# Sketched attention and a tanh feed-forward block on one core: engine orders from a searched table, w_out in 2 KB rows, part of the sketch set-up after the key projection

## The chip, the cores and the metric

The kernel runs on one core of a Trainium2 chip. The metric is the device time of one execution in microseconds (us); less is better. The kernel before was timed three times: 115.40, 114.22 and 115.14 us, median 115.14 us.

## What is computed

For each of 4 batches and 4 heads, with 1088 positions of 32 numbers, polynomial-sketch attention; its result, 4352 tokens of 128 numbers, goes through a feed-forward block of width 2048.

```python
def phi(x):                                   # r = 8, so 64 features
    a = np.einsum('rd,bhsd->bhsr', S1, x)
    b = np.einsum('rd,bhsd->bhsr', S2, x)
    return np.einsum('bhsi,bhsj->bhsij', a, b).reshape(*x.shape[:-1], r * r)
kv = np.einsum('bhsf,bhsd->bhfd', phi(k), v)
z = np.sum(phi(k), axis=2)
x = (phi(q) @ kv) / (phi(q) @ z + 1e-6)       # per head; heads side by side: 4352 x 128
h = x @ w_in                                  # 128 -> 2048
out = (h - np.tanh(h)) @ w_out                # 2048 -> 128
```

## The kernel before

Every operation is first recorded by `P.op` with an engine, an estimated cost, the tiles that it reads and writes, and a priority. `schedule` then simulates the five engines (TensorE = "tensor" or PE, ScalarE = "scalar" or ACT, VectorE = "vector" or DVE, GpSimd = "gpsimd" or POOL, SyncE = "sync" or SP) and puts each engine's operations in an order: of what is ready, the one of lowest priority number. `sync` puts semaphore waits between them. On the chip each engine runs its own list in that order, so an operation that waits holds up all that stand behind it on its engine.

The work has three layers. **Opening (batch 0).** Keys and queries are loaded, turned by DVE transposes (kT L496, qT L665), projected on PE with the sketch matrix psk (L503 "kproj", L685 "qproj"), and turned back (kab L515, qab L691). The outer products wk of the keys are formed on DVE and POOL (L555); PE sums them with v (L568 for batch 0, L637 for others). The denominators go through a fold (gram L523, zm L529, and either u0 at L730 or ufold L532 and u L703) and a DVE chain uT, dm, den, rden, qa; the outer products qp of the queries follow (L587, L786). PE turns qp (L602) and forms the numerators ("num": L619 for batch 0, in the pieces tiles 0, 1, 2-3, 4-7, 8; L809 for others), and ACT or DVE casts them into xT (L625, L819), which holds the tokens in bf16. **Weights.** w_in and w_out are loaded in four pieces each (L411, L416), cast to bf16 (w_in by ACT and POOL at L832, w_out by POOL at L836); w_in is turned on PE (L846, copied out by ACT at L851), and PE multiplies it with w_out into a 128 x 128 matrix, kept as whi and wlo ("wfold", L858). So h @ w_out needs only x times whi and wlo ("lin", L886). **Layers.** Ten windows of tokens (256, 256, seven of 512, 256) run over 16 blocks of the width 2048: PE multiplies xT with a block of w_in ("L1", L901), ACT takes tanh of two or four blocks at once, 1024 columns (L905, into one of 20 slots of tt), PE adds w_out times that into one PSUM bank ("L2", L914). At the end of a window DVE turns the bank (osb L920) and four to eight DMAs write it out. The hidden product uses PSUM banks 0 to 3 in two pairs; banks 1 to 3 serve the opening too: num of tiles 2-3 of batch 0 lies in bank 3 until DVE casts it into xT (L625, 128x256), and the second half of the fourth group of L1 needs that bank. Batches 1 to 3 of the attention are woven between the windows.

`schedule` also puts filler matmuls on PE (on the zero tile wz, L427 and L428), where PE would idle, from when the memset of wz (L426) stands in DVE's list until the first numerators.

## Time and profile before

| | |
|---|---|
| runs, us | 115.40, 114.22, 115.14 (median 115.14) |
| profiled execution, us | 114.93 |
| its span, first to last instruction, us | 113.1 |
| PE busy | 100.4 us, 89% |
| ACT busy | 76.3 us, 67% |
| DVE busy | 60.7 us, 54% |
| POOL busy | 35.6 us, 32% |

Times in the rows are us from the start of the span unless marked ns. In a timeline row the first number is the start, the second the time to the end of the last instruction of the group, xN the number of instructions, and the bracket the idle time of that engine just before and what ended it. Ends of matmuls are modelled, and matmuls overlap: "busy" of PE is more than its streaming. PEclk is the granted clock of PE as a share of 2.4 GHz.

### The profile page before, as it was taken

The numbers are of one execution on the slowest core, as the hardware profiler recorded it, in microseconds if no ns is written. First come the engines' busy times: TensorE is split into PE (matmuls) and PEld (weight loads), VectorE is DVE, ScalarE is ACT, GpSimd is POOL, SyncE is SP. The second block draws the span as 40 slices with busy tenths as digits, with TensorE's granted clock in tenths as the row PEclk, the third lists the DMA queues.
The fourth block names the chain that finished last, engine by engine and source line by source line (L and its number), as shares of the span: only waits on it lengthen the run. The fifth ranks groups of instructions, "written<-read, shape, count | busy, mean of one in ns | idle before, by whom it ended". The sixth has DMA issues, their size and how long they took to land.

```text
span 113.1 us, 2876 instructions
## 1 busy us (share of the span) xinstructions
PE 100.4 (89%) x1204; PEld 53.1 (47%) x1215; DVE 60.7 (54%) x150; ACT 76.3 (67%) x98; POOL 35.6 (32%) x43
## 2 busy tenths in 40 slices
PE   4999893599998979999999999999999989989770
PEld 3847552496546624343643434364344434335450
DVE  1679951997497973948973395398503020020210
ACT  3006395565543863949799677959977999999900
POOL 5528362040085850087670008729100000000000
PEclk9999999859999999999999999999999999999999
DMA  2999999400199311894300230060014033014053
GB/s 80 291 236 372 307 316 202 130 7 0 26 306 254 64 22 25 267 248 123 61 0 0 45 54 0 0 97 1 0 23 70 6 47 48 0 26 67 0 90 50
DMA packets 25724, 11.19 MB, mean 99 GB/s; under 512 B 18928, under 2 KB 23408, under 8 KB 25712
## 3 DMA queue, kind: packets, MB, share of 16 engines
q1 hardware_dynamic: 25136, 10.95, 40.8%
q8 instruction: 9, 0.15, 0.6%
q10 hardware_dynamic: 576, 0.07, 0.4%
q14 instruction: 3, 0.02, 0.1%
HBM read 8.78 MB, written 2.23 MB: 97 GB/s over the span
## 4 chain that ended last, share of the span: by engine, by line
PE 58%; DMA 13%; ACT 12%; DVE 6%; SPq 3%; issue 2%; POOL 2%; DVEq 0%
PE ps L901 20%; PE ps L914 18%; ACT tt L905 12%; DMA kraw<-in_k_dram 8%; DMA w_in_f<-in_moe_w_in_dram 5%; PE ps L809 4%; PE ps L886 4%; POOL qp L786 2%; PE ps L637 2%; DVE osb L920 2%; PE ps L703 2%; PE ps L685 2%; PE ps L503 2%; SPq L404 2%; PE ps L858 2%
## 5 line engine op out<-in xcount | busy, mean ns | idle before, releaser
L905 ACT ACTIVATE tt<-ps 128x1024 bf16<-128x1024 f32 (+1 forms) x70 | 66.2, 1003 | 14.1 <-PE ps L901 13.6
L901 PE MATMUL ps<-xT,w_in 128*128 128x512 bf16 (+1 forms) x155 | 40.8, 351 | 5.1 <-DVE xT L625 2.5
L914 PE MATMUL ps<-tt,w_out 128*128 128x512 bf16 (+1 forms) x154 | 38.4, 346 | 0.1
L555 POOL TENSOR_TENSOR wk<-kab 128x768 f32<-128x768 f32 (+2 forms) x11 | 15.7, 1423 | 27.6 <-DVE kab L515 24.3
L901 PEld LDWEIGHTS ps<-xT,w_in 128*128 128x128 bf16 x160 | 13.6, 98 | 21.1 <-ACT tt L905 9.2
L914 PEld LDWEIGHTS ps<-tt,w_out 128*128 128x128 bf16 x160 | 15.6, 99 | 14.4 <-issue 1.7
L920 DVE STREAM_TRANSPOSE osb<-ps 128x512 f32<-128x512 f32 (+1 forms) x10 | 6.3, 630 | 26.2 <-PE ps L914 19.2
L786 POOL TENSOR_TENSOR qp<-qa,qab 128x768 f32<-128x768 f32 x6 | 11.4, 1901 | 6.5 <-DVE qa L778 6.3
L792 DVE STREAM_TRANSPOSE qpT<-qp 128x768 f32<-128x768 f32 x9 | 8.8, 977 | 1.9 <-POOL qp L786 1.8
L496 DVE STREAM_TRANSPOSE kT<-kraw 128x576 f32<-128x576 f32 (+3 forms) x9 | 5.7, 663 | 2.4 <-DMA kraw<-in_k_dram 2.4
L819 DVE CAST xT<-ps 128x256 bf16<-128x256 f32 x6 | 2.5, 420 | 7.5 <-PE ps L809 7.5
L665 DVE STREAM_TRANSPOSE qT<-qraw 128x512 f32<-128x512 f32 (+1 forms) x8 | 5.6, 723 | 0.1
L819 ACT CAST xT<-ps 128x256 bf16<-128x256 f32 x6 | 2.2, 381 | 4.3 <-PE ps L809 4.3
L886 PE MATMUL ps<-xT,whi 128*128 128x512 bf16 (+1 forms) x10 | 3.5, 351 | 1.7 <-DVE osb L920 1.7
L809 PE MATMUL ps<-qpT,kvw 32*32 32x288 f32 (+1 forms) x192 | 4.6, 399 | 0.0
L691 DVE STREAM_TRANSPOSE qab<-ps 128x512 f32<-128x512 f32 (+1 forms) x5 | 3.0, 601 | 2.3 <-PE ps L685 2.2
L428 PE MATMUL ps<-wz 128*128 128x128 bf16 x25 | 3.2, 311 | 1.1 <-DVE pmask L443 1.1
L637 PE MATMUL ps<-wk,vx 128*32 128x64 f32 x216 | 3.6, 220 | 0.3 <-POOL wk L555 0.3
L637 PEld LDWEIGHTS ps<-wk,vx 128*32 128x32 f32 x216 | 3.2, 110 | 1.4 <-issue 1.4
L545 ACT COPY ps<-kab 128x128 f32<-128x128 f32 x1 | 0.3, 271 | 5.2 <-DVE kab L515 5.2
L836 POOL CAST w_out<-w_out_f 128x512 bf16<-128x512 f32 x4 | 2.5, 616 | 3.7 <-DMA w_out_f<-in_moe_w_out_dram 3.7
L886 PE MATMUL ps<-xT,wlo 128*128 128x512 bf16 (+1 forms) x10 | 3.5, 347 | 0.0
(110 smaller groups left out, 101.2 us busy)
## 6 DMA issues: line engine op xcount, KB each, us to landing
vx<-in_v_dram SPq DMA_DIRECT2D x8, 144.0 KB, 3.9
qraw<-in_q_dram SPq DMA_DIRECT2D x4, 288.0 KB, 5.6
qraw<-in_q_dram SPq DMA_DIRECT2D x4, 256.0 KB, 4.8
vx<-in_v_dram SPq DMA_DIRECT2D x8, 128.0 KB, 4.7
w_in_f<-in_moe_w_in_dram SPq DMA_DIRECT2D x4, 256.0 KB, 5.3
w_out_f<-in_moe_w_out_dram SPq DMA_DIRECT2D x4, 256.0 KB, 7.5
out_dram<-osb SPq DMA_DIRECT2D x16, 64.0 KB, 2.0
kraw<-in_k_dram SPq DMA_DIRECT2D x3, 288.0 KB, 2.7
```

Source lines behind the costliest of these rows:

```text
L496: P.op("vector", dve(hi - lo), lambda e, lo=lo, hi=hi: e.transpose(out=kT[:, lo:hi], in_=kraw[i][:, lo:hi]), r=cells("kraw", i, lo, hi), w ...
L555: P.op(eng, dve(cols) if eng == "vector" else pool2(cols), lambda e, t0=t0, t1=t1, ap=ap, m=m, ka0=ka0: e.tensor_tensor(out=wk[:, t0:t1, : ...
L637: ins = e.matmul(ps[32 * h:32 * h + 32, vb, 0:64], vx[i][:, h, t, :], wk[:, t, h, :, :], start=(t == 0), stop=(t == NT - 1), tile_position ...
L665: P.op("vector", dve(hi - lo), lambda e: e.transpose(out=qT[i][:, lo:hi], in_=qraw[i][:, lo:hi]), r=cells("qraw", i, lo, hi), w=cells("qT" ...
L786: P.op(eng, dve(cols) if eng == "vector" else pool2(cols), lambda e, p0=p0, p1=p1, w=w: e.tensor_tensor(out=qp[:, p0:p1, :, :, :].rearrang ...
L792: P.op("vector", dve(cols), lambda e, p0=p0, p1=p1: e.transpose(out=qpT[:, p0:p1, :, :, :].rearrange("p t h y j -> p (t h y j)"), in_=qp[: ...
L809: ins = e.matmul(ps[32 * h:32 * h + 32, nb[g], 0:32 * n], kvw[i][32 * g:32 * g + 32, y, 32 * h:32 * h + 32], qpT[32 * g:32 * g + 32, t0:t0 ...
L886: P.op("tensor", pe(n), lambda e, x=x: e.matmul(acc[:, 0:n], x[:, :], xT[:, f0:f0 + n], start=f0 > 0 and x is whi, stop=not f0 and x is wl ...
L901: P.op("tensor", pe(n), lambda e, jb=jb + y, y=y, hb=hb: e.matmul(hb[:, n * y:n * y + n], w_in[:, 128 * jb:128 * jb + 128], xT[:, f0:f0 + ...
L905: P.op("scalar", act(q * n), lambda e, un=un, hb=hb, q=q: e.activation(out=tt[:, un, 0:q * n], in_=hb[:, 0:q * n], func=AF.Tanh, scale=-1. ...
L914: P.op("tensor", pe(n), lambda e, jb=jb, un=un, y=y: e.matmul(acc[:, 0:n], w_out[:, jb, :], tt[:, un, n * y:n * y + n], start=(not f0 and ...
L920: P.op("vector", dve(n), lambda e: e.transpose(out=osb[u][:, 0:n], in_=acc[:, 0:n]), r=[ka], w=[("osb", u)], prio=slot0, name=f"osb{w}")
```

## The change

A table ORDER gives for each engine the numbers of the recorded operations in the order in which they run; `schedule` follows it and no longer chooses. Priorities and costs, several of which are changed too, no longer set an order; costs still decide where fillers go. In the vector list, operation 0, the memset of wz, is among the last entries (batch 3's part), and a filler may only be placed once it is listed; PE's list has none left (29 before). w_out is read so that a partition takes four consecutive rows (2 KB) instead of four rows 128 apart (512 bytes each); so that the product stays the same, the casts of w_in read their columns with a step of four. The mask and the matrix s2blk ("sketch", L456, L470, L459, L481 before) are made after the key projection. The fold of batch 0 comes after the sums. Of the copies of qpB, that of tile 1 moves to ACT and that of tiles 2-3 to DVE. No other arithmetic changes.

```diff
+ORDER = {
+    "tensor": (
+        "55 62 63 64 72 82 70 84 90 91 108 92 93 94 110 96 122 116 118 124 126 120 136 128 169 170 141 144 130 172 173 138 132 "
...
+    "vector": (
...
+        "494 518 515 517 0 514 519 520 521 522 532 533 531 575 529 535 602 604 603 633 680 731 775 "
...
+        turn = {}
+        for e, text in (ORDER or {}).items():
+            for x, i in enumerate(text.split()):
+                turn[self.ops[int(i)]] = x
...
+                if turn:
+                    o = min(avail[e], key=turn.get)
+                    t = max(free[e], o.ready)
...
     def load_w_out(prio):
         for x in range(4):
...
                 out=w_out_f[:, 4 * x:4 * x + 4, :],
-                in_=moe_w_out[512 * x:512 * x + 512, :].rearrange("(jb ji) c -> ji jb c", jb=4)))
+                in_=moe_w_out[512 * x:512 * x + 512, :].rearrange("(ji jb) c -> ji jb c", jb=4)))
...
     def casts(engs, gate):
...
-                w_in[:, 512 * x:512 * x + 512], w_in_f[:, 512 * x:512 * x + 512]),
+                w_in[:, 512 * x:512 * x + 512].rearrange("p (jb ji) -> p jb ji", jb=4),
+                w_in_f[:, 512 * x:512 * x + 512].rearrange("p (ji jb) -> p jb ji", jb=4)),
...
+    def folding(gate):
+        P.op("tensor", 60, lambda e: e.matmul(
+            ps[:, 6, 0:32], e4[:, :, :, :].rearrange("p a b c -> p (a b c)"), e4[:, 0, :, :].rearrange("p b c -> p (b c)"),
+            start=True, stop=True), r=[("e4",)], w=[bank[6]], prio=-898, mode="s", name="mask", ni=4, after=gate)
...
-    gram = keys(0, opening, (0, 1), 4)
+    gram = keys(0, opening, (0, 1), 4, then=folding)
...
+    key_fold(0, opening, 4, [summed])
...
-    x0 = numerators_first(first, [(1, 2, 3, "vector")], 6, "scalar")
+    x0 = numerators_first(first, [(1, 2, 3, "scalar")], 6, "scalar")
...
-    numerators_first(then, [(2, 4, 1, "scalar")], 3, "vector")
+    numerators_first(then, [(2, 4, 1, "vector")], 3, "vector")
```

**DVE, end of the opening.** Before, the transposes kT of batch 1's keys stand ahead of the cast of tiles 2-3 into xT (128x256):

```order
L665 STREAM_TRANSPOSE qT<-qraw 128x576
L691 STREAM_TRANSPOSE qab<-ps 128x2x4x2x16
L696 STREAM_TRANSPOSE qab<-ps 64x2x2x16
L711 STREAM_TRANSPOSE uT<-ps 128x128
L715 STREAM_TRANSPOSE uT<-ps 64x32
L496 STREAM_TRANSPOSE kT<-kraw 128x576
L625 CAST xT<-ps 128x256
L770 TENSOR_TENSOR dm<-qab,uT 128x20x8
L496 STREAM_TRANSPOSE kT<-kraw 128x512
```

and with the change (L552 is kT, L689 the cast, L651 qp):

```order
L729 STREAM_TRANSPOSE qT<-qraw 128x576
L673 COPY qpB<-ps 128x512
L755 STREAM_TRANSPOSE qab<-ps 128x2x4x2x16
L775 STREAM_TRANSPOSE uT<-ps 128x128
L760 STREAM_TRANSPOSE qab<-ps 64x2x2x16
L779 STREAM_TRANSPOSE uT<-ps 64x32
L834 TENSOR_TENSOR dm<-qab,uT 128x20x8
L837 TENSOR_REDUCE den<-dm 128x20
L689 CAST xT<-ps 128x256
L840 RECIPROCAL rden<-den 128x20
L842 TENSOR_TENSOR qa<-qab,rden 128x160
L651 TENSOR_TENSOR qp<-qa,qab 128x256
```

Both kT now stand behind these rows, so the cast no longer has a load of batch 1 ahead of it.

**POOL, casts of the weights.** Before, the four pieces of w_out are cast in the order of their loads (d_wo0 to d_wo3 are the semaphores of the pieces):

```order
L832 CAST w_in<-w_in_f 128x512 [waits s_gpsimd,s_scalar,d_wi2]
L832 CAST w_in<-w_in_f 128x512 [waits s_gpsimd,d_wi3]
L836 CAST w_out<-w_out_f 128x512 [waits s_gpsimd,d_wo0]
L836 CAST w_out<-w_out_f 128x512 [waits s_gpsimd,d_wo1]
L836 CAST w_out<-w_out_f 128x512 [waits s_gpsimd,d_wo2]
L836 CAST w_out<-w_out_f 128x512 [waits s_gpsimd,d_wo3]
```

and with the change (L896 casts w_in, L901 casts w_out):

```order
L896 CAST w_in<-w_in_f 128x512 [waits s_gpsimd,d_wi2,s_scalar]
L896 CAST w_in<-w_in_f 128x512 [waits s_gpsimd,d_wi3]
L901 CAST w_out<-w_out_f 128x512 [waits s_gpsimd,d_wo3]
L901 CAST w_out<-w_out_f 128x512 [waits s_gpsimd,d_wo2]
L504 MEMSET vx 64x4x32 [waits s_gpsimd]
L901 CAST w_out<-w_out_f 128x512 [waits s_gpsimd,d_wo0]
L901 CAST w_out<-w_out_f 128x512 [waits s_gpsimd,d_wo1]
```

The first cast now waits for the piece that is loaded last, and the piece that L2 needs first (d_wo0) comes third.

**PE, end of the program.** Before (L901 is L1, L886 lin, L914 L2; 128x256 is the last window):

```order
L901 MATMUL ps<-xT,w_in 128x256 x4
L914 MATMUL ps<-tt,w_out 128x512 x3
L901 MATMUL ps<-xT,w_in 128x256 x2
L914 MATMUL ps<-tt,w_out 128x512 x2
L901 MATMUL ps<-xT,w_in 128x256 x2
L886 MATMUL ps<-xT,whi 128x256
L886 MATMUL ps<-xT,wlo 128x256
L914 MATMUL ps<-tt,w_out 128x256 x16
```

and with the change (L966 is L1, L951 lin, L979 L2):

```order
L966 MATMUL ps<-xT,w_in 128x256 x4
L979 MATMUL ps<-tt,w_out 128x512 x3
L966 MATMUL ps<-xT,w_in 128x256 x6
L951 MATMUL ps<-xT,whi 128x256
L951 MATMUL ps<-xT,wlo 128x256
L979 MATMUL ps<-tt,w_out 128x256 x6
L966 MATMUL ps<-xT,w_in 128x256 x2
L979 MATMUL ps<-tt,w_out 128x256 x10
```

Six of the last window's sixteen L2 now stand ahead of its last two L1, ten behind them.

## Rows read from the trace of the kernel before

**Rows 1.** The head of the page: span, and busy time by engine.

```profile
span 113.1 us, 2876 instructions
PE 100.4 (89%) x1204; PEld 53.1 (47%) x1215; DVE 60.7 (54%) x150; ACT 76.3 (67%) x98; POOL 35.6 (32%) x43
```

**Rows 2.** The timeline, 19 to 25 us.

```profile
19.44 0.78 DVE L496 STREAM_TRANSPOSE kT<-kraw 128x576 f32<-128x576 f32 x1 [2.35 <-DMA kraw<-in_k_dram]
20.14 0.38 DVE L625 CAST xT<-ps 128x256 bf16<-128x256 f32 x1
20.59 0.83 PE L901 MATMUL ps<-xT,w_in 128*128 128x256 bf16 x6 [2.54 <-DVE xT L625]
...
22.92 1.91 PE L858 MATMUL ps<-w_out,w_inT 128*128 128x128 bf16 x16
```

**Rows 3.** Busy time by engine in stretches, with granted clock and DMA.

```profile
core 0: us, PE busy (x) PEld busy (x) DVE busy (x) ACT busy (x) POOL busy (x), PEclk, DMA share, GB/s
...
8.00:12.00 4.00, 4.00 (x119) 2.82 (x118) 3.84 (x15) 2.51 (x7) 3.28 (x5) 1.00 1.04 353
...
21.72:25.13 3.41, 3.04 (x23) 2.79 (x24) 3.31 (x8) 2.64 (x4) 1.55 (x2) 0.50 0.03 12
```

**Rows 4.** The timeline, 4 to 15 us, and one row at 29.7 us.

```profile
4.78 1.25 PE L428 MATMUL ps<-wz 128*128 128x128 bf16 x10
...
5.66 0.28 DVE L481 TENSOR_TENSOR s2blk<-ps,mask 128x128 f32<-128x128 f32 x1
...
5.95 1.19 PE L503 MATMUL ps<-kT,psk 64*32 64x288 f32 x16
...
13.13 0.42 DVE L609 COPY qpB<-ps 128x256 f32<-128x256 f32 x1
...
14.41 0.59 ACT L851 COPY w_inT<-ps 128x512 bf16<-128x512 bf16 x1
14.41 0.39 PE L901 MATMUL ps<-xT,w_in 128*128 128x256 bf16 x2
...
29.74 0.69 PE L503 MATMUL ps<-kT,psk 64*32 64x288 f32 x16
```

**Rows 5.** The timeline of POOL, 9 to 20 us.

```profile
10.96 1.36 POOL L832 CAST w_in<-w_in_f 128x512 bf16<-128x512 f32 x2 [0.36 <-DMA w_in_f<-in_moe_w_in_dram]
...
17.82 0.62 POOL L836 CAST w_out<-w_out_f 128x512 bf16<-128x512 f32 x1 [0.89 <-DMA w_out_f<-in_moe_w_out_dram]
```

**Rows 6.** DMA packets in 8:11 (w_in's) and in 12:14 (w_out's).

```profile
DMA packets 598, 1.08 MB, mean 358 GB/s; under 512 B 67, under 2 KB 91, under 8 KB 598
...
DMA packets 1185, 0.60 MB, mean 302 GB/s; under 512 B 36, under 2 KB 1184, under 8 KB 1184
```

**Rows 7.** The chain that ended last: start, us, what.

```profile
42.12 0.43 PE ps L914 x2
42.55 1.48 PE ps L809 x49
...
62.56 1.48 PE ps L809 x49
...
83.42 1.48 PE ps L809 x49
...
107.75 1.76 PE ps L914 x16
...
109.54 0.45 DVE osb L920
```

**Rows 8.** The timeline, 30 to 42 us.

```profile
30.74 0.67 DVE L515 STREAM_TRANSPOSE kab<-ps 128x512 f32<-128x512 f32 x1
...
40.87 0.39 PE L886 MATMUL ps<-xT,whi 128*128 128x512 bf16 x1 [0.75 <-DVE osb L920]
```

**Rows 9.** The timeline of ACT, 86 to 108 us.

```profile
86.33 14.14 ACT L905 ACTIVATE tt<-ps 128x1024 bf16<-128x1024 f32 x15 [0.61 <-PE ps L901]
100.67 6.75 ACT L905 ACTIVATE tt<-ps 128x1024 bf16<-128x1024 f32 x8 [0.20 <-PE ps L901]
```

## The prediction

> **What bounds the kernel now.** I read the head of the page first [rows 1]. PE is busy for 89% of a span of 113.1 us and every other engine for at most 67%, so an operation that another engine does sooner pays only where PE waits for it. The chain that ended last says the same [rows 7]: from about 21 us on nearly every piece is a matmul. It also gives the pitch, 0.43 us for two products of 512 columns (0.216 each) and 1.76 us for sixteen of 256 (0.11 each), and marks for stages: the first numerators by L809 (batch 1) at 42.55, batch 2 at 62.56, batch 3 at 83.42, the last L2 over at 107.75 + 1.76 = 109.51.

> Then I looked for the places where PE does wait. The largest is at the end of the opening [rows 2]. The transpose kT of batch 1 sits on DVE until its load lands at 19.44; the cast into xT that stands behind it, and needs nothing of it, starts at 20.14; PE idles 2.54 us and resumes at 20.59. After that idle the granted clock is 0.50, the lower level of 1.2 GHz, from 21.72 to 25.13, while PE is busy for 3.04 of 3.41 us [rows 3]. The wfold (16 products of 128 columns, at 22.92) lies in that stretch. Smaller waits are the one for osb before lin, 0.75 us [rows 8], and those at the end, where ACT runs 15 and 8 tanh groups nearly without a gap from 86.33 to 107.42 [rows 9], so that there ACT is as much a bound as PE.

> Before about 15 us DVE is the bound: it is busy for 3.84 of 4 us between 8 and 12 [rows 3].

> The sum is made on the profiled execution, 114.93 us, of which 1.83 lie outside the span. The median of the runs, 115.14, is 0.2 higher.

> **The change part by part: the opening, to the wfold.** The cast into xT is taken out from behind kT, as the order in the section on the change shows. Counted from DVE's own durations, what stands ahead of it now ends near 18 us. DVE gets s2blk (0.28) and the like small copy of the mask inside its busy stretch, and loses the 0.42 copy of qpB to ACT [rows 4]: about even. PE gets two small products (mask, s2p) ahead of the query projection, behind which DVE still has kab to do. ACT now copies a w_inT (0.59) ahead of the second cast into xT, so the first L1, at 14.41 before [rows 4], comes some 0.9 later. ACT hides that: it then has three full groups' worth of work until about 20 us.

> What is late next is w_out. POOL now waits for the last piece first and casts the others behind it. Before, the last piece landed at 17.82 [rows 5]. Its 1.05 MB moved at 302 GB/s in 512-byte packets; w_in's 2 KB packets moved at 358 [rows 6], which is 3.5 against 2.9 us, 0.55 sooner: 17.25. [...] Four casts of 0.62 follow, 2.5 us, with a small memset among them, as an estimate 0.2: 2.7 us, so the wfold starts at 20.0 instead of 22.92: **-2.9 us**.

> The casts of w_in with a step of four are not in the trace. The nearest row is the plain cast, 1.36 us for two on POOL [rows 5]; they may cost the same or up to twice that (and as much on ACT). I take the same, because POOL then has its work done by 12.3, and even at double by 13.7, ahead of w_out's landing, which hides it. [...]

> **Filler.** All 29 filler matmuls go. I cost that at +0.4 us inside the opening, hidden by w_out. The reason: kproj took 1.19 us at 5.95, although ten fillers ran just ahead of it, and 0.69 at 29.74 [rows 4]; ten fillers of 128 columns took 1.25. So PE was slow at 6 us with the filler too, and what filler bought is the time between about 8 us and the point at which the real work alone brings the clock up. DVE bounds that part.

> **From the wfold to the first numerators of batch 1.** Before this took 42.55 - 22.92 = 19.63 us. By the order the change has 55 products of 256 columns and 19 of 512 there (L1, L2 and lin), against 48 and 19: +0.77. No half clock there: 2.21 us of the slow stretch fell into it, half comes back, -1.1. Of the wait for osb (0.75) I take half back, since twelve ready L2 stand behind lin now; -0.4. So 18.9, **-0.7 us**, and num of batch 1 starts at 38.9. For that kab of batch 1 (30.74 before) must start 3.6 us sooner; its kT is now done near 21 and PE is the one that it waits for.

> **From there to the numerators of batch 3.** 40.87 us before, with 132 products of 512 columns (L1, L2, lin); the change has 134: **+0.4 us**, 41.3. PE streams without long gaps in this stretch and the attention's own products are the same, so an order can give little. 80.2.

> **The end.** 26.09 us before. ACT's list has the same 21 full groups and two half ones behind the casts of batch 3, so its run takes the same 21.1 us. But sixteen L2 of 0.11 stood behind the last lin; now ten stand behind the last L1, of which eight can run beside the last tanh. ACT ended at 107.42 and PE 2.09 later; I expect about 0.5 to 0.7 later: **-1.4 us**. Bounds: -0.4 (87 against 85 products of 512 columns, if PE decides) and -1.6. L2 is over at 80.2 + 26.1 - 1.4 = 104.9.

> Behind it stay 3.6 us of span (osb 0.45, the last DMAs) and 1.83 outside: 110.3. Check by terms: 114.93 - 2.9 - 0.7 + 0.4 - 1.4 = 110.3.

> **The rivals.**

> *PE stays at the lower clock through the opening (slower).* Without the filler, the work that is left is sparse until 15 us. For it: the only drop in the profile follows an idle stretch of PE [rows 2, 3]. Against it: from 5.95 on real products came at nearly every moment, and at double length they fill PE more. Price: 20 L1 at 0.21 instead of 0.11 (+2.0), the wfold 1.91 instead of half of that (+1.0), the transposes of qp, the numerators and the projections of batch 0, which the slow stretch shows at about double (+2.5), and +0.5 in the chain of DVE: 6 us, that is 116.3. It decides if the granted clock is still 0.50 when the stream gets dense, at about 20 us; up to some 15 us DVE and the loads hide most of it. [...]

> *Given back midway.* The new order often issues one L1, one L2, one L1, so that a late tanh stops PE at once; before, the waits of PE were few. If each of the three woven batches loses 0.8 us so, and w_out lands no sooner (0.55), 110.3 + 2.4 + 0.55 = 113.3. For it: L1 and tanh alternate on two pairs of banks. Against it: ACT has slack (67%) [rows 1].

> *More than that.* All of the osb waits go, w_out lands 1.1 us sooner and the first L1 isn't later: -0.55, -0.4, and about 1.8 of waits for tanh and osb in the middle: 107.5. For it: the attention pieces of a batch are free to move. Against it: the middle is dense already.

> **How the numbers follow.** My forecast, 110.3, has a chance of 0.53 (108.5 to 111.8), "more" 0.20, "given back" 0.18, "lower clock" 0.09. The range reaches down to "more", 107.2, and up past "given back", 114.0. What a measurement of this kernel tells from no change is about 1%, that is outside 114.0 to 116.3. The forecast and "more" are faster, "given back" mostly; "lower clock" is split between the same and slower, and I leave some for stalls that I don't see: faster 0.83, same 0.09, slower 0.08.

> **What would show it.** Right: the cast into xT (L689) starts near 18 us, with no kT ahead of it; the wfold (L923) near 20 us, its release a cast by POOL; no granted clock of 0.50 after 20 us; num (L873) of batch 1 near 39, of batch 3 near 80; ACT's last tanh and the last L2 within 0.8 us of each other. Wrong: kproj, q projection and the transposes of qp of batch 0 at double length beyond 15 us; a wait of PE for tanh above 0.5 us in each batch; the wfold later than 21 us; a w_in cast on ACT that holds up qpB.

## The result and the profile after

The changed kernel took 110.73 us (median of 4 executions, 109.54 to 111.58) against 114.92 us before (median of 4, 114.22 to 115.40): ratio 0.9605, 95% interval 0.9503 to 0.9707. It is faster by about 4%, and the time is within half a microsecond of the 110.3 that was predicted. The terms behind the sum are another matter: the one that was to carry most of it failed in part, and others took its place.

The profiled execution of the changed kernel is the longest of its four, 111.58 us, so its opening, read below, is longer than that of the median. How much can be told, because what follows the wfold repeats: execution less start of the wfold is 88.57 us here and 88.53 to 88.77 in the other kernels below that have the changed order (89.25 where its end was put back). By that the median execution began its wfold at about 110.73 - 88.57 = 22.16 us (an estimate, which takes it that its later stages repeat too). Every ratio here leaves out the executions that took over 1.5% longer than the fastest of their kernel (the 111.58 is one), while the medians count all.

In the changed kernel L966 is L1, L979 L2, L951 lin, L923 the wfold, L689 the cast into xT, L873 num, L552 kT, L559 kproj and L985 osb. Marks of the two profiled executions, in us:

| | before | after | difference of the stage | predicted |
|---|---|---|---|---|
| first L1 | 14.41 | 19.25 | | some 15.3 |
| wfold | 22.92 | 23.01 | +0.1 | -2.9 |
| num of batch 1 | 42.49 | 40.99 | -1.6 | -0.7 |
| num of batch 3 | 83.35 | 81.45 | -0.4 | +0.4 |
| last tanh ends | 107.42 | 105.60 | | |
| last L2 ends | 109.50 | 106.06 | -1.5 | -1.4 |
| span | 113.1 | 109.8 | | 108.5 |

The head of the page of the changed kernel (for [rows 1]):

```profile
span 109.8 us, 2823 instructions
PE 98.8 (90%) x1176; PEld 52.2 (48%) x1186; DVE 60.7 (55%) x150; ACT 77.5 (71%) x98; POOL 36.6 (33%) x43
```

PE is busy 1.6 us less, part of it the fillers that are gone; the other engines are busy as long as before or longer. The other 1.7 of the 3.3 us by which the span is shorter are time in which PE stood idle. The waits of PE, changed kernel (what waited, what for, us in total, times, longest):

```profile
PE ps L512 <- DMA s_raw<-in_S_dram: 3.6, 1, 3.6
PE ps L559 <- DVE kT L552: 1.3, 1, 1.3
PE ps L966 <- issue: 0.6, 4, 0.2
PE ps L794 <- DVE zm L587: 0.4, 1, 0.4
...
PE ps L640 <- ACT kvs L637: 0.3, 1, 0.3
PE ps L873 <- DVE qpT L856: 0.2, 1, 0.2
```

and of the kernel before:

```profile
PE ps L901 <- DVE xT L625: 2.5, 1, 2.5
PE ps L886 <- DVE osb L920: 1.7, 3, 0.8
PE ps L901 <- ACT tt L905: 1.3, 4, 0.5
```

Its three large waits behind 18 us (for xT, osb and tanh, 5.5 us together) are gone; the first two rows of the changed kernel lie ahead of 5.3 us, where PE waits for the first loads and keys and the kernel before ran fillers. Behind that the list names no new wait of their size (0.4 and 0.3 us in the opening, 0.2 for qpT), and yet the wfold came no earlier. Behind 5.3 us PE hardly waits in the opening, it works slowly. Its timeline there (for [rows 2, 4]; start, us, instructions):

```profile
5.26 1.18 PE L559 MATMUL ps<-kT,psk 64*32 64x288 f32 x16 [1.33 <-DVE kT L552]
...
8.05 1.22 PE L787 MATMUL ps<-qT,s2rep 128*128 128x256 f32 x2
...
19.25 0.62 PE L966 MATMUL ps<-xT,w_in 128*128 128x256 bf16 x2
...
20.84 0.38 PE L966 MATMUL ps<-xT,w_in 128*128 128x256 bf16 x2
...
23.01 1.05 PE L923 MATMUL ps<-w_out,w_inT 128*128 128x128 bf16 x16
```

The same key projection takes 0.69 us at the full clock [rows 4], and the same two L1 0.62 us at 19.25 but 0.38 at 20.84. By these lengths PE works at about half speed until just before 20 us; the trace's first record of a granted clock of 1.0 stands at 19.73. In the kernel before, that record stands at 8.07. What half speed is, the wfold shows: in the chain that ended last its sixteen products of 128 columns take 1.71 us at 23.13 in the kernel before, at a granted clock of 0.50 [rows 3], and 0.89 us at 23.17 in the changed kernel, at 1.0. That is 1.2 columns per ns against 2.3, and the 512 columns in 0.216 us of the prediction [rows 7] are 2.4; these are the rates behind the 1.2 and 2.4 GHz of the recorded texts.

DVE then reaches the cast only at 21.94 (for the DVE rows of [rows 2]):

```profile
20.41 0.45 DVE L755 STREAM_TRANSPOSE qab<-ps 128x256 f32<-128x256 f32 x1 [0.65 <-PE ps L749]
...
21.94 0.42 DVE L689 CAST xT<-ps 128x256 bf16<-128x256 f32 x1
...
23.28 1.36 DVE L552 STREAM_TRANSPOSE kT<-kraw 128x576 f32<-128x576 f32 x2
```

No kT stands ahead of it any more, as predicted; DVE waits for PE's products instead. POOL (for [rows 5]) shows that w_out was not what came late next:

```profile
11.16 2.37 POOL L896 CAST w_in<-w_in_f 128x512 bf16<-128x512 f32 x2 [0.57 <-DMA w_in_f<-in_moe_w_in_dram]
15.98 1.36 POOL L901 CAST w_out<-w_out_f 128x512 bf16<-128x512 f32 x2 [2.45 <-DMA w_out_f<-in_moe_w_out_dram]
...
17.73 1.36 POOL L901 CAST w_out<-w_out_f 128x512 bf16<-128x512 f32 x2
```

The last cast of w_out is over at 19.1, almost 4 us ahead of the wfold. The casts of w_in with a step of four take 2.37 us for two instead of 1.36. The last two groups of the chain that ended last (for [rows 7]) and ACT's end (for [rows 9]):

```profile
104.96 1.11 PE ps L979 x10
106.16 0.45 DVE osb L985
```

```profile
88.10 16.71 ACT L970 ACTIVATE tt<-ps 128x1024 bf16<-128x1024 f32 x18
105.00 0.60 ACT L970 ACTIVATE tt<-ps 128x512 bf16<-128x512 f32 x1 [0.20 <-PE ps L966]
```

The last L2 now ends 0.46 us behind the last tanh (106.06 and 105.60), 2.08 before.

### The profile page after: what moved, and what is told of

Read it like the earlier page. It is cut to its first block, busy times and chain, and to the rows that moved or that the text cites. A ratio compares the mean times of both kernels' runs of the same rounds, so it can differ in the third digit from the quotient of the medians.

```text
span 109.8 us, 2823 instructions
## 1 busy us (share of the span) xinstructions
PE 98.8 (90%) x1176; PEld 52.2 (48%) x1186; DVE 60.7 (55%) x150; ACT 77.5 (71%) x98; POOL 36.6 (33%) x43
## 4 chain that ended last, share of the span: by engine, by line
PE 68%; ACT 14%; DVE 6%; POOL 3%; DMA 2%; issue 2%; ACTq 1%; DVEq 0%
PE ps L979 19%; PE ps L966 18%; ACT tt L970 14%; PE ps L873 4%; POOL qp L850 3%; PE ps L666 3%; PE ps L749 3%; PE ps L559 3%; PE ps L683 3%; PE ps L787 2%; PE ps L701 2%; PE ps L951 2%; DMA s_raw<-in_S_dram 2%; PE ps L631 2%; PE ps L767 1%
## 5 line engine op out<-in xcount | busy, mean ns | idle before, releaser
L966 PE MATMUL ps<-xT,w_in 128*128 128x512 bf16 (+1 forms) x151 | 40.3, 348 | 1.0 <-issue 0.6
L979 PE MATMUL ps<-tt,w_out 128*128 128x512 bf16 (+1 forms) x160 | 39.7, 347 | 0.3 <-issue 0.3
L979 PEld LDWEIGHTS ps<-tt,w_out 128*128 128x128 bf16 x160 | 15.5, 98 | 13.7 <-issue 0.9
L966 PEld LDWEIGHTS ps<-xT,w_in 128*128 128x128 bf16 x160 | 14.4, 100 | 15.7 <-ACT tt L970 5.8
L985 DVE STREAM_TRANSPOSE osb<-ps 128x512 f32<-128x512 f32 (+1 forms) x10 | 6.3, 630 | 22.7 <-PE ps L979 22.7
L552 DVE STREAM_TRANSPOSE kT<-kraw 128x576 f32<-128x576 f32 (+3 forms) x9 | 5.6, 659 | 1.1 <-DMA kraw<-in_k_dram 1.1
L873 PE MATMUL ps<-qpT,kvw 32*32 32x288 f32 (+1 forms) x192 | 4.6, 398 | 0.2 <-DVE qpT L856 0.2
L559 PE MATMUL ps<-kT,psk 64*32 64x288 f32 (+1 forms) x64 | 3.2, 465 | 1.3 <-DVE kT L552 1.3
L666 PE MATMUL ps<-ident,qp 128*128 128x128 f32 (+1 forms) x18 | 3.8, 341 | 0.0
L573 DVE STREAM_TRANSPOSE kab<-ps 128x512 f32<-128x512 f32 (+1 forms) x5 | 2.9, 591 | 1.6 <-PE ps L559 1.6
L916 ACT COPY w_inT<-ps 128x512 bf16<-128x512 bf16 x4 | 2.3, 585 | 2.0 <-PE ps L911 1.9
L951 PE MATMUL ps<-xT,wlo 128*128 128x512 bf16 (+1 forms) x10 | 3.5, 347 | 0.2 <-issue 0.2
L873 PEld LDWEIGHTS ps<-qpT,kvw 32*32 32x32 f32 x192 | 2.5, 103 | 2.3 <-issue 0.8
```

The costliest lines, as they stand in the source:

```text
L559: ins = e.matmul(ps[32 * g:32 * g + 32, kb[r], 0:n], psk[64 * r:64 * r + 64, :, :, :].rearrange("p a h i -> p (a h i)"), kT[64 * r:64 * r ...
L666: ins = e.transpose(out=ps[:, tb, at:at + n], in_=qp[0:n, t, 2 * x:2 * x + 2, :, :].rearrange("p h i j -> p (h i j)"), identity=ident[0:n, ...
L873: ins = e.matmul(ps[32 * h:32 * h + 32, nb[g], 0:32 * n], kvw[i][32 * g:32 * g + 32, y, 32 * h:32 * h + 32], qpT[32 * g:32 * g + 32, t0:t0 ...
L966: P.op("tensor", pe(n), lambda e, jb=jb + y, y=y, hb=hb: e.matmul(hb[:, n * y:n * y + n], w_in[:, 128 * jb:128 * jb + 128], xT[:, f0:f0 + ...
L979: P.op("tensor", pe(n), lambda e, jb=jb, un=un, y=y: e.matmul(acc[:, 0:n], w_out[:, jb, :], tt[:, un, n * y:n * y + n], start=(not f0 and ...
L985: P.op("vector", dve(n), lambda e: e.transpose(out=osb[u][:, 0:n], in_=acc[:, 0:n]), r=[ka], w=[("osb", u)], prio=slot0, name=f"osb{w}")
```

## The experiments

Times below are medians; a ratio is to the kernel before, on the same chip, with its 95% interval. "Opening" is the start of the wfold in the profiled execution.

**1. The filler given back.** The memset of wz goes from the end of DVE's list to its start, so that `schedule` places 45 filler matmuls in PE's gaps: 39 of 128 columns ahead of the key projection, 6 of 256 between 8.7 and 12.2 us.

```diff
     "vector": (
-        "12 13 14 7 17 15 ...
+        "0 12 13 14 7 17 15 ...
...
-        "494 518 515 517 0 514 ...
+        "494 518 515 517 514 ...
```

> The changed kernel with the memset of wz put first in DVE's list again, so that the scheduler places fillers (46 on PE before the first numerators); all else in the changed order. Theory A (the lower clock holds the opening of the changed kernel): PE at 2.4 GHz by about 8 us instead of 19.7, first L1 near 16 instead of 19.25, wfold near 20.5 instead of 23.0, time 2 to 3 us below the changed kernel. Rival (DVE, the step-4 casts or the loads hold the opening whatever the clock): first L1 within 1 us of 19.25, time within 0.7 us of the changed kernel.

109.08 us, ratio 0.9434 (0.9368 to 0.9500); profiled 109.42 us. PE's timeline:

```profile
5.32 0.69 PE L559 MATMUL ps<-kT,psk 64*32 64x288 f32 x16 [0.15 <-DVE kT L552]
...
15.87 0.38 PE L966 MATMUL ps<-xT,w_in 128*128 128x256 bf16 x2
...
20.11 0.28 PE L979 MATMUL ps<-tt,w_out 128*128 128x256 bf16 x1 [0.62 <-POOL w_out L901]
20.86 1.07 PE L923 MATMUL ps<-w_out,w_inT 128*128 128x128 bf16 x16 [0.47 <-POOL w_out L901]
```

and DVE's cast:

```profile
18.63 0.41 DVE L689 CAST xT<-ps 128x256 bf16<-128x256 f32 x1
```

With filler PE is at its full clock from the key projection on (clock record from 4.38), the first L1 is 3.4 us earlier, the cast starts at 18.63, and the wfold at 20.86 is released by a cast on POOL. That is the opening as the prediction described it, 0.9 us late: the last piece of w_out is cast from 17.55 on, not 17.25, and the four casts are over at 20.81, 3.3 us behind that instead of 2.7. The description needed a PE at full clock, and the change had taken that away. Without the filler the changed kernel loses some 1.65 us (medians; 2.15 in the two profiles). The two intervals only just part; experiment 4 makes the same comparison once more.

**2. The filler taken from the kernel before.** One name in L427 is changed, so that `schedule` finds no filler.

```diff
-        P.filler = (lambda e: e.matmul(
+        fillers = (lambda e: e.matmul(
```

> The kernel before without its 29 fillers, every list else as before. Theory (the wait for batch 1's keys, until 19.4 us, gives the opening of the kernel before slack, so filler is worth little there): PE at half clock well past 8 us, first L1 2 to 4 us later than 14.4, but the wfold less than 1.5 us later than 22.9, time 0 to 1 us above the kernel before. Rival (filler is worth the same in both orders): time 2 us or more above.

115.00 us, ratio 0.9999 (0.9964 to 1.0035): no change. Yet PE was slow for longer: two products for bq (L723) still take 1.22 us at 10.40, 0.70 at 8.81 in the kernel before (clock record from 16.66, against 8.07 and, in a second profile of the kernel before, 12.22; first L1 at 18.01). DVE's rows tell why:

```profile
20.52 0.16 DVE L715 STREAM_TRANSPOSE uT<-ps 64x32 f32<-64x32 f32 x1
20.62 0.72 DVE L496 STREAM_TRANSPOSE kT<-kraw 128x576 f32<-128x576 f32 x1
21.27 0.37 DVE L625 CAST xT<-ps 128x256 bf16<-128x256 f32 x1
```

With filler, DVE sat 2.35 us in front of kT [rows 2]; without it the slower chain arrives at 20.6, when the keys have landed, and the wait of 2.35 us is used up. The wait for the keys hid the cost of the low clock. In this execution it did not hide all of it: kT starts at 20.62 without a wait for its load, and the wfold, at 24.20, is later than in both profiles of the kernel before (22.92 and 23.64); the execution, 115.70 us, lies above the median of its kernel. With filler the wfold follows the keys: in three profiles of the old order (two of the kernel before, one in experiment 8) the first kT starts at 19.44, 20.42 and 18.61 and the wfold at 22.92, 23.64 and 21.83, while the first L1 stands at 14.41, 16.36 and 14.75. The change removed the wait and the filler together, and so uncovered a cost that the filler had never been seen to save.

**3. The wait for the keys taken from the kernel before.** Only the two kT of batch 1 are gated behind the cast (L625); lists and filler follow.

```diff
-            gate = () if b == 1 else gate
+            gate = P.writer[("x", 0, 2, 0)] if b == 1 else gate
```

> The kernel before with one thing changed: kT of batch 1 stands behind the cast into xT on DVE (filler, PE, ACT, POOL and SP lists as before). Theory (the stall is worth what the prediction put on it): no wait of 2.5 us on PE at 18 to 20.6 us, no clock of 0.50 at 21.7, wfold near 20, time 2.5 to 3.7 us below the kernel before. Rival (what is lost there is hidden, since the DVE chain, w_out and later stages end as late): less than 1 us.

114.72 us, ratio 0.9974 (0.9936 to 1.0012): no change that can be told. A second profile of it beside one of the kernel before:

> e4_xfirst profiled once more (its first profile had the clock up only at 14.0 us). Theory: the wfold now follows the first L1, since nothing else waits for a load: with the clock up near 8 us, first L1 near 14.4 and wfold 21 to 22; with the clock up near 14, first L1 near 17.8 and wfold near 24.2. Rival (ACT's and DVE's work between decides): wfold near 24 in both.

> The kernel before, profiled once more. Theory (its wait for batch 1's keys takes up whatever the opening loses to the clock): if the clock comes up later than 8 us here, the first L1 is later than 14.4, the wait of PE before 20.6 is shorter by as much, and the wfold is within 1.3 us of 22.9. Rival (the opening sets the later stages): the wfold shifts by as much as the first L1.

114.71 and 115.56 us. The rows of the second profile of this version, DVE and PE:

```profile
19.65 0.42 DVE L625 CAST xT<-ps 128x256 bf16<-128x256 f32 x1
```

```profile
21.26 0.61 PE L901 MATMUL ps<-xT,w_in 128*128 128x256 bf16 x4 [0.46 <-ACT tt L905]
22.66 0.61 PE L901 MATMUL ps<-xT,w_in 128*128 128x256 bf16 x4 [0.53 <-ACT tt L905]
23.23 1.05 PE L858 MATMUL ps<-w_out,w_inT 128*128 128x128 bf16 x16
```

and of the kernel before beside it:

```profile
20.42 0.78 DVE L496 STREAM_TRANSPOSE kT<-kraw 128x576 f32<-128x576 f32 x1 [1.38 <-DMA kraw<-in_k_dram]
21.12 0.38 DVE L625 CAST xT<-ps 128x256 bf16<-128x256 f32 x1
```

ACT of this version:

```profile
20.18 1.02 ACT L905 ACTIVATE tt<-ps 128x1024 bf16<-128x1024 f32 x1 [0.79 <-PE ps L901]
21.10 0.58 ACT L851 COPY w_inT<-ps 128x512 bf16<-128x512 bf16 x1
21.56 1.04 ACT L905 ACTIVATE tt<-ps 128x1024 bf16<-128x1024 f32 x1
22.48 0.61 ACT L851 COPY w_inT<-ps 128x512 bf16<-128x512 bf16 x1
```

Here the cast starts 1.5 us sooner, but from cast to wfold it takes 3.58 us (23.23 - 19.65) instead of 2.52 (23.64 - 21.12). Behind the cast ACT still has two tanh and two copies of w_inT to do, one after another, and the wfold needs the last copy; in the profile of before the first of each pair started at 19.60 and 20.52, while PE stood still. Freed of the stall, PE meets ACT. In both profiles of this version the clock rose at 13.6 to 14.0 us, in those of before at 8.1 and 12.2. So the stall that I read as 2.54 us of loss was worth at most 0.7 us (the lower end of the interval) in the old order. Whether the old order would gain with a clock that rises at 4 us was not tried.

**4. Rows of w_out.** The changed kernel with 512-byte rows and plain casts again (two things at once), without filler; and both this and the filler.

```diff
-                in_=moe_w_out[...].rearrange("(ji jb) c -> ji jb c", jb=4)))
+                in_=moe_w_out[...].rearrange("(jb ji) c -> ji jb c", jb=4)))
...
-                w_in[:, ...].rearrange("p (jb ji) -> p jb ji", jb=4),
-                w_in_f[:, ...].rearrange("p (ji jb) -> p jb ji", jb=4)),
+                w_in[:, ...], w_in_f[:, ...]),
```

> The changed kernel with w_out again in 512-byte rows and w_in cast without a step; order and missing filler as changed. Theory A: casts back at 0.62 us each on ACT and POOL (1.15 and 1.19 in the changed kernel), the last w_out piece back at about 17.8 us (16.0 in the changed kernel), but both lie beside PE's slow work, which releases the wfold only near 23: time within 0.5 us of the changed kernel. Rival (the step-4 casts hold ACT and by it the first L1): first L1 and time 1 us or more sooner.

> Both: filler as in e1_fill and rows and casts as in e2_rows. If the 2 KB rows are worth something once the clock is up, w_out lands last here (17.8 us, casts over near 20.5, wfold after 20.5) and this kernel is 0.5 to 1.5 us slower than e1_fill. If the step-4 casts on ACT hold the warm opening, it is 0.5 us or more faster than e1_fill.

110.05 us, ratio 0.9560 (0.9505 to 0.9615), and 110.99 us, ratio 0.9516 (0.9438 to 0.9594). In the second, three of six executions had a mean granted clock of 0.984 or 0.985 and took 111.5 to 112.3 us; the other three took 108.96 to 110.45. Neither can be told from its partner (0.9605 and 0.9434). Nor can the two be told from each other, though only the filler parts them. Their profiles show the filler as experiment 1 does (wfold at 22.34 without and 20.41 with it, executions of 110.87 and 108.96 us), but the medians stand the other way round, by the three executions at a lower clock. So the time that the filler saves is shown by one pair of kernels and not by the other. POOL of the version without filler:

```profile
11.23 1.35 POOL L896 CAST w_in<-w_in_f 128x512 bf16<-128x512 f32 x2 [0.33 <-DMA w_in_f<-in_moe_w_in_dram]
16.12 1.64 POOL L901 CAST w_out<-w_out_f 128x512 bf16<-128x512 f32 x2 [3.54 <-DMA w_out_f<-in_moe_w_out_dram]
```

The first cast waits for the last piece in both kernels: 16.12 us in 512-byte rows, 15.98 in 2 KB rows. From 12 to 14 us DMA did move 386 GB/s with the long rows and 300 with the short ones:

```profile
DMA packets 413, 0.77 MB, mean 386 GB/s; under 512 B 46, under 2 KB 46, under 8 KB 412
```

```profile
DMA packets 1209, 0.60 MB, mean 300 GB/s; under 512 B 41, under 2 KB 1208, under 8 KB 1209
```

(the changed kernel first), but the last piece's landing differs by 0.14 us here and by 1.6 us between two kernels with the same rows (15.98 and 17.55 with filler). The gain of the rate does not show in the time. With plain casts on both sides, experiment 5 has the 2 KB rows and the second kernel here the short ones: 0.9464 and 0.9516, not told apart, the last piece cast from 16.73 and 17.15.

**5. The step of four in PE's weight loads.** Experiment 1, with plain casts; the turns of w_in and the 160 L1 read their 128 weights with the step instead.

```diff
+    def block(jb):
+        x, j = divmod(jb, 4)
+        return w_in[:, 512 * x:512 * x + 512].rearrange("p (ji jb) -> p jb ji", jb=4)[:, j, :]
...
-                    hb[:, n * y:n * y + n], w_in[:, 128 * jb:128 * jb + 128], xT[:, f0:f0 + n], ...
+                    hb[:, n * y:n * y + n], block(jb), xT[:, f0:f0 + n], ...
```

> e1_fill with plain casts of w_in; the step of four is put into PE's weight loads instead (turns of w_in and all 160 L1 read their 128 columns with a step of 8 bytes). If weight loads hide a step, casts fall from 1.12 to 0.62 us each, the opening ends 0.3 to 0.8 us sooner, and the time is 0 to 0.8 us below e1_fill. If the step makes weight loads longer than a product of 512 columns hides, every L1 pays and the time is 3 us or more above.

108.81 us, ratio 0.9464 (0.9419 to 0.9510): not told from experiment 1. ACT's casts fall back from 1.13 to 0.62 us each and the wfold goes from 20.86 to 20.05, still released by POOL's casts of w_out (waits of 0.60 and 0.46 us). That step of 0.81 us is w_out's, not the casts': its last piece is cast from 16.73 on, 0.82 us sooner than in experiment 1. The stages behind the wfold are 0.02 to 0.07 us longer each. The step costs PE next to nothing, and the doubled casts were hidden, as predicted.

**6. Casts of w_out in the order of their loads.** Experiment 1, with POOL's four casts in the order 0, 1, 2, 3 and the memset of vx behind them.

```diff
-        ... 102 103 107 106 24 104 105 ...
+        ... 102 103 104 105 106 107 24 ...
```

> e1_fill with POOL casting the pieces of w_out in the order of their loads, and the memset of vx behind them. Theory (the cast of the last piece standing first holds the first L2 and the wfold once the opening is at full clock): first cast before 16.5 us, first L2 and wfold 0.5 to 1.3 us sooner than 20.1 and 20.9, time 0.4 to 1 us below e1_fill. Rival (ACT's tanh and DVE's qa decide as well): within 0.3 us.

108.56 us, ratio 0.9434 (0.9382 to 0.9487).

```profile
14.56 2.12 POOL L901 CAST w_out<-w_out_f 128x512 bf16<-128x512 f32 x3 [0.79 <-DMA w_out_f<-in_moe_w_out_dram]
16.87 0.61 POOL L901 CAST w_out<-w_out_f 128x512 bf16<-128x512 f32 x1 [0.19 <-DMA w_out_f<-in_moe_w_out_dram]
```

The casts are over at 17.5 instead of 20.8, PE's waits for them vanish, and the wfold starts at 19.8. That is 1.1 us in the profile (109.42 to 108.34), which the ratios don't show (0.9434 both). So in the profile of experiment 1 the order "last piece first" of the change's table does hold the wfold, once PE is fast enough to meet it. How much depends on the landing: it was late there (17.55), and in the profile of experiment 7, with the same order, the casts start at 16.06, are over at 19.4 and hold nothing.

**7. The end of PE's list as before.** Experiment 1, with the last two L1 ahead of lin and all sixteen L2 behind.

```diff
-        ... 752 757 758 759 760 761 762 763 764 754 755 765 ...
+        ... 752 754 755 757 758 759 760 761 762 763 764 765 ...
```

> e1_fill with the end of PE's list as in the kernel before: the last two L1 ahead of lin, all sixteen L2 of the last window behind it; all else as e1_fill. Theory (the end is worth what the prediction put on it): the last L2 over 1.8 to 2.2 us after the last tanh instead of 0.46, time 1.2 to 1.7 us above e1_fill. Rival (ACT or osb sets the end): within 0.4 us of e1_fill.

110.08 us, ratio 0.9497 (0.9443 to 0.9550); one of the six executions took 130.13 us, at a mean granted clock of 0.757. PE's end:

```profile
102.82 0.39 PE L966 MATMUL ps<-xT,w_in 128*128 128x256 bf16 x2 [0.65 <-ACT tt L970]
103.05 0.27 PE L951 MATMUL ps<-xT,whi 128*128 128x256 bf16 x1
...
103.26 1.91 PE L979 MATMUL ps<-tt,w_out 128*128 128x256 bf16 x16
```

From num of batch 3 to the end of the last L2 it takes 25.28 us instead of 24.61: +0.67. The last L2 ends 1.33 us behind the last tanh, not 2.08 as in before; lin no longer waits for osb there (0.58 us at 107.36 before). The time itself can't be told from experiment 1 (0.9434); the stage is what shows it. The opening of this execution is 0.6 us later than that of experiment 1 (wfold at 21.46) in spite of the filler: the clock, up at 5.46, was back at 0.50 from 8.87 to 12.28. Of the 1.5 us that the end gained, about 0.7 is the order at the end of the list; the other 0.9 is the size of the two waits for osb that before had in this stretch and the changed kernel has not:

```profile
99.60 0.39 PE L886 MATMUL ps<-xT,whi 128*128 128x512 bf16 x1 [0.35 <-DVE osb L920]
...
107.36 0.28 PE L886 MATMUL ps<-xT,whi 128*128 128x256 bf16 x1 [0.58 <-DVE osb L920]
```

That they are its cause was not tested.

**8. One wait for osb taken from the kernel before.** In DVE's list osb of the second window goes ahead of the second transposition qpT of batch 1 (its lines stand 3 higher).

```diff
+        v = order["vector"]
+        i = next(i for i, o in enumerate(v) if o.name == "osb1")
+        v[i - 1], v[i] = v[i], v[i - 1]
         return order
```

> The kernel before with one exchange in DVE's list: the turn of the second window's L2 bank (osb, L920) goes ahead of the second transposition qpT of batch 1 (L792), which it followed. In before, PE waited 0.75 us for that osb ahead of lin at 40.87. Read by one stage, the key projection of batch 1 to its first numerators, 12.75 us in before (29.74 to 42.49) and 12.74 without the filler. Theory (the wait is a term of its own, as the prediction has it): lin starts some 0.6 us sooner after the L1 ahead of it; the last qpT still starts when POOL's product for it is there, so the numerators may wait 0.1 to 0.4 for it; stage 12.1 to 12.4, execution 0.3 to 0.6 us shorter (ratio 0.995 to 0.997). Rival one (the wait only covers the chain qp, qpT of DVE and POOL, which sets the numerators anyway): PE's wait moves to the numerators in full, stage 12.65 to 12.8. Rival two (the exchange delays the second qpT and with it the numerators): stage 13.0 or more. In the changed kernel no wait for osb is left at all, and its stage from the key projection to the numerators is 12.33 us (28.66 to 40.99) with four products of 512 columns' worth of L2 fewer or more, so the theory also says what that stage owes to this one place.

114.65 us, ratio 0.9994 (0.9956 to 1.0033).

```profile
39.04 0.39 PE L889 MATMUL ps<-xT,whi 128*128 128x512 bf16 x1
...
41.03 1.55 PE L812 MATMUL ps<-qpT,kvw 32*32 32x288 f32 x64 [0.31 <-DVE qpT L795]
```

The wait of 0.75 us at lin is gone, 0.31 of it comes back at the numerators, and the stage from the key projection (28.65) to them is 12.38 us instead of 12.75. In the profile the wait was half loss and half cover for DVE and POOL, as the theory had it; the execution time does not resolve the 0.37 us.

**9. Experiments 1, 5 and 6 together.**

> e1_fill with both e7_step_weights and e9_castorder: plain casts of w_in, the step in PE's weight loads, w_out cast in the order of its loads. If the casts of w_out are what releases the wfold in e7 (20.05) and the first L1 what does it in e9 (16.24, wfold 19.78), the two together bring the wfold to 18.8 to 19.4 and the time to 107.3 to 108.2 us. If DVE's qa and ACT's tanh decide anyway, it stays at 108.3 to 108.8.

107.72 us, ratio 0.9401 (0.9345 to 0.9458), the lowest median of all, though its interval overlaps those of experiments 1, 5 and 6; its profiled execution took 107.56 us.

```profile
span 105.8 us, 2923 instructions
PE 99.4 (94%) x1231; PEld 55.1 (52%) x1231; DVE 59.9 (57%) x150; ACT 76.3 (72%) x98; POOL 35.6 (34%) x43
```

The wfold starts at 18.79 us, 4.2 earlier than in the changed kernel, and the span is 4.0 shorter.

## Why the prediction came out as it did

The marks of the opening, side by side (us; "clock" is where the record of 1.0 begins, "cast" is the first cast on DVE into xT):

| | clock | first L1 | cast | wfold | execution |
|---|---|---|---|---|---|
| before | 8.07 | 14.41 | 20.14 | 22.92 | 114.93 |
| before, second profile | 12.22 | 16.36 | 21.12 | 23.64 | 115.56 |
| before, no filler | 16.66 | 18.01 | 21.27 | 24.20 | 115.70 |
| before, cast ahead of kT | 13.98 | 17.78 | 20.60 | 24.19 | 115.61 |
| before, osb sooner (experiment 8) | 8.70 | 14.75 | 19.31 | 21.83 | 113.41 |
| after | 19.73 | 19.25 | 21.94 | 23.01 | 111.58 |
| after, 512-byte rows | 16.90 | 18.81 | 21.26 | 22.34 | 110.87 |
| after, filler | 4.38 | 15.87 | 18.63 | 20.86 | 109.42 |
| after, filler, 512-byte rows | 4.67 | 15.06 | 17.52 | 20.41 | 108.96 |
| after, filler, end as before (experiment 7) | 5.46, 0.50 again 8.87 to 12.28 | 17.93 | 20.38 | 21.46 | 110.71 |
| experiment 9 | 4.76 | 15.24 | 17.69 | 18.79 | 107.56 |

**The opening, -2.9: wrong in part.** The profile shows +0.1; for the median execution it is some -0.8 (22.16 against 114.92 - 91.97 = 22.95, by the 92.01 and 91.92 us that follow the wfold's start in the two profiles of before). The step that failed is the one on the filler: "I cost that at +0.4 us inside the opening, hidden by w_out". By experiment 1 it measured about 1.65 us (1.9 to 2.2 in the profiles of two pairs; the medians of the second pair do not show it) and was not hidden. Its ground, a key projection that was slow in spite of ten fillers, holds in the profile of before and in the first of experiment 3 (1.19 us each, with 29 fillers). What it missed is what the filler does behind that, as the table shows: with 29 fillers the clock rose at 8 to 14 us, with none at 16.7 to 19.7, with 45 at 4.38 to 5.46 (the four kernels of the table that have them, though in experiment 7 it fell once more, to 0.50 from 8.87 to 12.28). The words that DVE and the loads "hide most of it" until 15 us held for the kernel before only, where the wait for batch 1's keys absorbed the rest, and that wait was the very thing that the change removed. What comes late next was named as w_out; it was the chain of PE, at half speed, and DVE. Two of the prediction's own signs of being wrong came: the transposes of qp at 17.91 take 1.12 us for four (0.66 with filler), and the wfold is later than 21. The lower-clock rival had the mechanism, at too high a price (6 us): it took nearly every matmul of the opening as doubled and on the path. Of the twenty L1 and the wfold, which it priced at 3.0 us, only the first two L1 ran slow: the clock rose at 19.73, and the wfold took 1.05 us.

The three groups of start times stand in the order of the filler, and in two pairs filler is all that differs: 19.73 without and 4.38 with it in the changed order (experiment 1), 16.66 against 8.07 and 12.22 in the old one (experiment 2). So in these runs more filler went with an earlier rise, and without any the clock rose at 16.66 to 19.73; by what rule PE is granted the clock no run shows. The 116.3 us did not come, for the reason just given.

**The casts with a step, taken as plain and hidden: size wrong, sum right.** They take 1.09 to 1.15 us each on POOL and ACT against 0.61 and 0.62, some 1.8 times, near the upper bound of twice. Experiment 5 shows the cover.

**The rows of w_out, -0.55: not shown.** The rate rose, and more than worked out (386 GB/s, 358 forecast). The last piece was cast from 15.98 on, sooner than the 17.25 forecast and than the 16.7 that "more than that" comes to (1.1 us before 17.82); but with 512-byte rows that is 16.12, so the rows explain 0.14 us of it at most. In the two profiles of the kernel before it is 17.82 and 18.65; what made it sooner is not shown.

**From the wfold to num of batch 1, -0.7: right in sign, -1.6 measured.** Two terms were off. The half clock cost less than the 1.1 us put back: in the profiles of the old order without a drop (two of experiment 3, one of experiment 2, the second of the kernel before) the stage takes 19.07 to 19.48 us against 19.57, so 0.1 to 0.5. And PE's waits are gone in full: the 0.75 us for osb, of which I took half, and 0.30 us for wk of POOL. In the changed order the 72 sums of batch 1 stand between the last L2 of a window and lin, and DVE turns the bank meanwhile. The three profiles with 19.07 us hold a third wait, 0.50 us for qpB of DVE (26.65 in the second of experiment 3), which is gone too; a wait of 0.21 us for qpT at 40.99 is new. The waits come to 1.34 us less and the seven more products to 0.77 more, while the stage is 1.09 shorter than 19.07: 0.5 us is unexplained. That the waits are the cause is read from their sizes; the one for osb, taken away by itself in experiment 8, was worth 0.37 in the stage, the half that was booked.

**From there to num of batch 3, +0.4: -0.4 measured.** Two waits for tanh of 0.25 us are gone, against 0.21 us for qpT; that gives -0.3 beside the two more products (+0.43), so 0.5 us is unexplained here too. "Given back midway" did not occur: the list of waits has none for tanh left. The alternation of L1 and L2, which I counted as a danger, goes with fewer waits, not more.

**The end, -1.4: -1.5 measured.** Right in sum and in its sign (last tanh and last L2 within 0.46 us); by experiment 7 half of it came by the order at the end, and the other half has the size of two waits for osb that I had not booked (not tested). So the order was worth 0.7 us, not the 1.4 booked.

So the total was right by luck: an opening about 2 us worse than forecast was met by 0.9 us more behind the wfold, 0.8 us more in the middle and 0.1 at the end, for other reasons, about 1 us of which is unexplained. "More than that" came nearest to what happens behind the opening.

## What to carry to other kernels

A wait is worth what is late next, and that is known only once the speed of what stood in its shade is known: one stall can hide a slow engine, and a measure that buys nothing beside the stall (here the filler, 0.9999) may be worth something without it (here 1.7% in one pair of kernels and 0.4%, not told from nothing, in another). So when a change removes a stall and something that looks useless in the same stroke, test them apart. Read the clock from durations of like instructions, not from one row of one execution, and test whether stages repeat between executions: where everything behind one mark does, the spread lies ahead of it.

## What was not expected of the hardware

```profile
8.00:12.00 4.00, 3.62 (x62) 2.26 (x54) 3.19 (x14) 0.64 (x2) 3.21 (x4) 1.00 1.03 360
```

(the changed kernel; the two products at 8.05 take 1.22 us there and 0.70 with filler). The landing of w_out's last piece moved by more than 1.5 us between kernels with the same loads in the same order (15.98 and 17.55), and by 0.8 us between two executions of the kernel before (17.82 and 18.65).
